# Linear attention and eight experts on one core: the step order up to chunk 7 written anew, and when expert 3's scales and the raw tiles are worked on

## The chip, the cores and the metric

The kernel runs on one core of a Trainium2 chip as one program. The metric is the device time of one execution in microseconds (us). Names of engines: PE is TensorE (PEld its weight loads), DVE is VectorE, ACT is ScalarE, POOL is GpSimd, SP is SyncE, which here only issues DMAs.

## The reference

Two stages follow each other. The first is gated linear attention over 4 batches, 8 heads, 768 tokens and 48 channels a head; the second passes its output through 8 experts, weighted by a Sinkhorn-normalised gate:

```python
def _attn_ref(q, k, v, alpha):              # each [4, 8, 768, 48]
    for t in range(S):
        state = alpha[:, :, t, :, None] * state + einsum('bhd,bhe->bhde', k[:, :, t], v[:, :, t])
        y[:, :, t] = einsum('bhd,bhde->bhe', q[:, :, t], state)

def _moe_ref(x, w_gate, w1, w2):            # x [3072, 384], w1 [8, 384, 1024], w2 [8, 1024, 384]
    logits = x @ w_gate
    P = exp(logits - logits.max())
    for _ in range(8):
        P /= P.sum(1, keepdims=True) + 1e-09
        P /= P.sum(0, keepdims=True) + 1e-09
        P *= N / E
    for e in range(E):
        out += P[:, e:e + 1] * (maximum(x @ w1[e], 0.0) @ w2[e])
```

## The kernel before

**Attention.** The 3072 tokens (4 batches of 768) are 24 chunks of 128 and 12 units of 256 (two chunks). Chunks 0 to 3 are worked directly (`direct_chunk`, 12 steps each); from unit 2 on, `attn_block` (16 steps and a DMA step) prepares a unit: it loads q, alpha and k (`qt`, `al`, `kt`), forms products within groups of 16 tokens on POOL (`tmp`), sums them on DVE into `AB`, multiplies decays into `qt`, `kt`, `al`, and writes all of it to DRAM and back in another layout (`ks`, `qs`, `ds`, `As`, then `KN`, `QN`, `DN`, `an`). That write-back is the last step, 13 DMAs on SP. `attn_decays` turns `DN` on PE (`psd`) into the decay tables (`dT`, `q32`, `k32` and others); `attn_chunk` (5 steps) turns K and Q (`psk`, `psq`), multiplies in the tables (`decq`, `deck`, on DVE), forms the scores on PE (`psl`), copies them out on ACT (`A`), and `attn_tail` forms the output (`psy`), scales it by its maximum (`mx`, then four one-column operations to `s_t`, all on DVE, then `ys` on ACT), turns it (`psx`) and splits it into two half-precision parts (`xT`: ACT the high part, DVE the low one). A chunk is done for the experts when its `xT` is written. Names carry batch and chunk: chunk 4 is `0_4`, chunk 5 `0_5`, chunk 6 `1_0`, chunk 7 `1_1`, chunk 8 `1_2`; blocks of units 2, 3, 4 are `0_2`, `1_0`, `1_1`.

**Experts.** Each product of the second stage is three half-precision matmuls (`PASSES`). `moe_tile` takes 256 tokens (512 later) of one expert: 8 hidden tiles (`ps1`, 9 matmuls each, evacuated by ACT into `h0` and by DVE into `h1`), then an output tile for each 128 tokens (`ps2`, 24 matmuls). PSUM holds four such tiles. `load_expert` loads a weight matrix, squares it on ACT (`junk`, four pieces), sums over partitions on PE (`pst_w1`, `pst_w2`), derives a power of two on DVE (`root_scale`, six small operations) and splits the weights in four pieces (`w10`/`w11`, `w20`/`w21`).

**Order.** Experts 0 to 2 (NA = 3) run beside the attention: their tiles stand in the list `filler`, and `fill(us)` takes that many us of matmuls from it. Their outputs go to DRAM unscaled (`evac_raw`, tensors `raw0` to `raw2`), since the gate is known only after all chunks. Up to chunk 7 (and two steps of chunk 8) the order is written out by hand in the string START: `c3` is a step of chunk 3, `b2` one of unit 2's block, `w1` one of expert 1's weights, `d2` the decays of unit 2, `g` the gate's weights, `f` a `fill(0.45)`, which does nothing while the list is empty. A capital letter gives more work to POOL: in `B`, the first product of the block's last level (`tmp8`, 128x1536) runs on POOL and not on DVE; in `W`, a piece's low part is formed on POOL. PE always keeps the order in which the program is written; up to the end of the Sinkhorn phase so do DVE, ACT, POOL and SP (`hold`). From chunk 8 on, a planner interleaves steps with `fill(4.7 / 2)`.

**After the attention** comes the Sinkhorn phase, a chain of small DVE operations and one matmul an iteration (`pssk`) among filler; then the rest of the list, in which expert 3's weights are scaled, one step after each `fill(1.0)`; then experts 3 to 7 in turn. Expert 3 reads all three raw tiles of its 128 tokens back (`ri`, pool `rp` of three buffers) and adds them, scaled by the gate (`evac_first`); the others only add their own output (`evac_add`).

Of the kernel before, what the change touches and what calls it, by code (L numbers as in the profile page):

```python
# [23 lines left out]
def tile_gla_moe(ctx: ExitStack, tc: tile.TileContext, q, k, v, alpha, wg, w1, w2, out):  # L24
    nc = tc.nc
    B, H, S, D = q.shape
    NT, DM = out.shape
    E, _, FF = w1.shape
    P = 128
# [6 lines left out]
    NP = H // 2  # L36
    DP = 64
    OFF = 28
    START = 'c0 c1 f c0 f f f c1 W0 w0 f f c0 f c1 f f f f f w0 c0 f f W0 w0 f f f f f f c0 f f f c1 w0 f w0 c1 c0 f f f f w1 f w0 f f w0 f f w0 c1 w0 f w0 W1 f f c0 c2 f f f c2 f c1 f g c1 c0 c3 f f c1 f f W0 c0 f W0 f w0 f c2 c3 f f c1 f c1 f W0 c0 g c2 f w1 f f c0 W1 f f c3 w1 g f f c2 W1 f c3 c2 c1 f f f c3 w1 w0 f f f c2 f f f w1 c3 f f f c2 f f f f f f f w1 c3 f f W1 c3 f w1 f f f f f f f f f c3 w1 f c2 w1 b2 w1 w1 f f f W1 f c2 f f b2 f f f f f f c2 f f f f f f B2 f w1 f B2 f c2 c3 f f f b2 f f f f c3 c3 f f f f B2 f B2 b2 f f f f f f f f B2 f f f f f f f f f f f f f b2 f f b2 f f B2 B2 B2 f f f f b2 f f B2 f f f f f f f f f f f f f f f f c4 d2 f f f f f c4 f f f B3 b3 f f b3 c0 c4 f f f f f b3 b3 b3 b3 b3 f f f f f b3 w2 c5 f f f f f b3 f f f f f b3 w2 c4 f f f f f f b3 f f f f f b3 w2 c5 f f f f f b3 f f f f f b3 w2 c4 f f f f f f b3 f f f f f w2 c5 f f f f f f f f f f w2 d3 c6 f f f f f f f f f f f b4 w2 c5 f f f f f b4 f f f f f b4 w2 c6 f f f f f b4 f f f f f f b4 w2 c5 f f f f f b4 f f f f f b4 w2 c6 f f f f f b4 f f f f f b4 w2 c7 f f f f f f b4 f f f f f b4 w2 c6 f f f f f b4 f f f f f b4 w2 c7 f f f f f f b4 f f f f f b4 w2 c6 f f f f f b4 f f f f f w2 c7 f f f f f f f f f f f w2 d4 c8 f f f f f f f f f f b5 c7 f f f f f b5 f f f f f f b5 c8 f f f f f b5 f f f f f b5 c7 f f f f f b5 f f f f f b5'.split()
    FILL = 4.7  # L40
    NA = 3

# [20 lines left out]
    VE, SE, GE, SP = (Held(x) for x in (nc.vector, nc.scalar, nc.gpsimd, nc.sync))  # L63
# [4 lines left out]
    def tr(out_, in_, idn):  # L68
# [4 lines left out]
    sm = ctx.enter_context(tc.tile_pool(name="sm", bufs=4))  # L73
# [40 lines left out]
    def root_scale(sq, target, nm):  # L114

        g = sm.tile([P, 1], F32, tag="rs_g", name=f"g_{nm}")
        VE.tensor_reduce(g, sq, axis=AX.X, op=ALU.add)
        VE.tensor_scalar_max(g, g, 1e-30)
        p = sm.tile([P, 1], F32, tag="rs_p", name=f"p_{nm}")
        VE.tensor_scalar(p.bitcast(I32), g.bitcast(I32), 24, 23,  # L120
                         op0=ALU.logical_shift_right, op1=ALU.logical_shift_left)
        VE.tensor_scalar_mul(p, p, 2.0 ** 64)
        r = sm.tile([P, 1], F32, tag="rs_r", name=f"r_{nm}")
        VE.tensor_scalar(r.bitcast(I32), p.bitcast(I32), EXPM, None, op0=ALU.bitwise_xor)
        sc = sm.tile([P, 1], F32, tag="rs_s", name=f"s_{nm}")
        VE.tensor_scalar_mul(sc, r, target / 2)
        return p, sc
# [32 lines left out]
    def load_expert(e, pool, res):  # L160

        todo, pws = [], []
        for nm, w, target, C, W in (("w1", w1, W1T, KT_, FF), ("w2", w2, W2T, FT, DM)):
            src = w[e].rearrange("(c p) f -> p c f", p=P)
            hl = [(wpa[0] if e == NA - 1 else wp).tile([P, C, W], F16, tag=f"{nm}{i}", name=f"{nm}{i}_{e}")
                  for i in range(2)]
            res.append(hl)
            hl = [x.rearrange("p c w -> p (c w)") for x in hl]
            if pool is None:

                r = 1 if nm == "w1" else 2
# [535 lines left out]
    def fill(us):  # L707
        owed[0] += us
        while owed[0] > 0 and filler:
            try:  # L710
                owed[0] -= next(filler[0])
            except StopIteration:
                filler.pop(0)
        if not filler:
            owed[0] = 0.0

    def advance(gen, n):
        for _ in range(n):
            next(gen, None)
# [162 lines left out]
    advance(w3_, 99)
    hold[0] = False
# [3 lines left out]

    T = 512

    def evac_first(e, tt, ps):  # L890
        for i in range(NA):
            r = rp.tile([P, DM], F32, tag="raw", name=f"ri{i}_{tt}")
            SP.dma_start(r, raw[i][tt * P:(tt + 1) * P])
            pt = sm.tile([P, 1], F32, tag="pe0", name=f"pe{i}_{tt}")
            VE.tensor_mul(pt, PR[:, tt, i:i + 1], wsc[:, i:i + 1])
            if i == 0:
                SE.activation(acc[:, tt], r, AF.Copy, scale=pt)
            else:
                VE.scalar_tensor_tensor(acc[:, tt], r, pt, acc[:, tt], op0=ALU.mult, op1=ALU.add)
# [44 lines left out]
```

## Time and profile before

| | us |
|---|---|
| three runs, median (lowest to highest) | 1843.33 (1843.16 to 1844.97) |
| the profiled execution | 1843.05 |
| its span, first to last instruction | 1841.3 |
| around the span | 1.75 |
| PE busy | 1745.6 |
| DVE, ACT, POOL busy | 840.4, 541.9, 297.4 |

A row of the timeline gives start, duration, engine, line, operation, output<-inputs, shape and count, and in brackets how long that engine had sat idle just before and what released it. Line numbers say little here, since nearly all operations are recorded through the two helpers at lines 57 and 66; tiles are told apart by name and place in time. A row of the table by stages gives the stage, its length, and for each engine busy time and instruction count; PEclk is the granted PE clock as a share of full speed.

### The profile page before, as it was taken

How to read it: one execution, taken by the hardware profiler on the slowest of the kernel's cores; microseconds unless marked ns; L12 is line 12 of the kernel's file. 1: busy time of each engine (PE TensorE's matmuls, PEld its weight loads, DVE VectorE, ACT ScalarE, POOL GpSimd, SP SyncE). 2: the span in 40 equal slices, each digit the busy share in tenths (PEclk: the TensorE clock that was granted, in tenths of full speed). 3: DMA queues.
4: the chain of work that ended last, by engine and by line, in shares of the span. 5: the costliest groups of instructions: out<-in, count | busy, mean ns of one | idle time of the engine just before them, and what ended most of it. 6: DMA issues, size and time to landing. Idle time of an engine off the chain costs nothing.

```text
span 1841.3 us, 34101 instructions
## 1 busy us (share of the span) xinstructions
PE 1745.6 (95%) x14774; PEld 1132.8 (62%) x14774; DVE 840.4 (46%) x1851; ACT 541.9 (29%) x1221; POOL 297.4 (16%) x270
## 2 busy tenths in 40 slices
PE   5899488999999999998999999999999999999999
PEld 5776466777777777776554555555555555555555
DVE  6465576666566556336465233222422242222222
ACT  5453243334333333325442123111411121111111
POOL 1124444445335424200000000000000000000000
PEclk9999598999999999999999999999999999999999
DMA  6114503431330432022362002000200000000000
GB/s 174 37 41 97 145 21 82 98 74 44 94 93 19 102 94 62 25 95 78 123 195 86 1 1 69 1 1 1 69 1 1 1 1 1 1 1 19 34 18 35
DMA packets 148198, 98.13 MB, mean 53 GB/s; under 512 B 107216, under 2 KB 138192, under 8 KB 148048
## 3 DMA queue, kind: packets, MB, share of 16 engines
q1 hardware_dynamic: 148048, 95.95, 18.8%
q8 instruction: 116, 1.90, 0.4%
q14 instruction: 34, 0.28, 0.1%
HBM read 67.63 MB, written 28.30 MB: 52 GB/s over the span
## 4 chain that ended last, share of the span: by engine, by line
PE 78%; DVE 10%; ACT 4%; DMA 4%; issue 2%; POOL 1%; SPq 0%; ACTq 0%; DVEq 0%; POOLq 0%
PE ps L66 70%; PE psy L66 3%; PE psl L66 2%; DMA ri<-raw 2%; DVE AB L57 2%; POOL tmp L57 1%; DVE tmp L57 1%; DVE deck L57 1%; DVE decq L57 1%; DVE h L57 1%; PE pss L66 1%; DVE w L57 1%; ACT junk L57 1%; ACT w L57 1%; ACT A L57 1%
## 5 line engine op out<-in xcount | busy, mean ns | idle before, releaser
L66 PE MATMUL ps<-xT,w 128*128 128x256 f16 (+2 forms) x4824 | 777.8, 320 | 16.8 <-DVE h L57 13.1
L66 PE MATMUL ps<-w,h 128*128 128x384 f16 x4608 | 774.1, 327 | 10.7 <-DVE h L57 9.8
L66 PEld LDWEIGHTS <-w 128*128 128x128 f16 x4824 | 467.7, 99 | 304.7 <-issue 20.1
L66 PEld LDWEIGHTS <-h 128*128 128x128 f16 x4608 | 450.0, 98 | 306.0 <-issue 9.7
L57 ACT ACTIVATE h<-ps 128x256 f16<-128x256 f32 (+2 forms) x536 | 251.6, 475 | 800.1 <-PE ps L66 799.6
L57 DVE SCALAR_TENSOR_TENSOR h<-ps,h 128x256 f16<-128x256 f32 (+2 forms) x536 | 280.9, 537 | 434.6 <-ACT h L57 434.2
L57 DVE SCALAR_TENSOR_TENSOR acc<-ps,pe,acc 128x384 f32<-128x384 f32 x120 | 74.1, 617 | 307.6 <-PE ps L66 307.6
L57 POOL TENSOR_TENSOR tmp<-qt,kt 128x768 f32<-128x768 f32 (+2 forms) x81 | 141.5, 1752 | 153.1 <-DVE AB L57 66.0
L57 DVE TENSOR_REDUCE AB<-tmp 128x16 f32<-128x768 f32 (+2 forms) x90 | 81.1, 902 | 42.0 <-POOL tmp L57 41.8
L57 ACT COPY r<-ps 128x384 f32<-128x384 f32 x72 | 34.4, 477 | 149.4 <-PE ps L66 139.7
L57 ACT COPY A<-psl 16x128 f32<-16x128 f32 (+4 forms) x164 | 52.5, 327 | 53.4 <-PE psl L66 51.9
L66 PE MATMUL psy<-vn,A 128*128 128x48 f32 x384 | 58.2, 283 | 1.7 <-issue 1.7
L66 PE MATMUL psl<-Tq,Tk 48*32 48x16 f32 (+3 forms) x2752 | 46.1, 191 | 13.9 <-DVE A L57 6.0
L66 PEld LDWEIGHTS psy<-vn,A 128*128 128x128 f32 x384 | 54.9, 209 | 2.1 <-issue 2.0
L66 PEld LDWEIGHTS psl<-Tq,Tk 48*32 48x32 f32 (+2 forms) x2752 | 40.7, 114 | 23.9 <-issue 8.7
L57 ACT ACTIVATE ys<-psy,s_t 128x384 f32<-128x384 f32 x24 | 14.0, 581 | 104.0 <-DVE s_t L57 79.4
L57 POOL TENSOR_TENSOR kt<-kt,al 128x384 f32<-128x384 f32 x40 | 41.1, 1028 | 2.6
L57 POOL TENSOR_TENSOR A<-an,mask 128x1024 f32<-128x1024 f32 x20 | 40.0, 2000 | 0.0
L57 DVE TENSOR_TENSOR qt<-qt,al 128x384 f32<-128x384 f32 (+1 forms) x50 | 39.6, 792 | 0.0
L57 DVE SCALAR_TENSOR_TENSOR acc<-ri,pe,acc 128x384 f32<-128x384 f32 x48 | 29.5, 616 | 21.4 <-DMA ri<-raw 18.3
L57 DVE TENSOR_REDUCE mx<-psy 128x1 f32<-128x384 f32 x24 | 13.3, 555 | 56.7 <-PE psy L66 56.7
L66 PE MATMUL psy<-ST,Tq 128*128 128x96 f32 x160 | 35.6, 306 | 2.9 <-DVE lg L57 1.8
(160 smaller groups left out, 965.0 us busy)
## 6 DMA issues: line engine op xcount, KB each, us to landing
raw<-r SPq DMA_DIRECT2D x72, 192.0 KB, 1.9
ri<-raw SPq DMA_DIRECT2D x72, 192.0 KB, 2.4
w1f<-in_moe_w_dram SPq DMA_DIRECT2D x5, 1536.0 KB, 6.4
w2f<-in_moe_w_dram SPq DMA_DIRECT2D x5, 1536.0 KB, 7.3
vn<-in_v_dram SPq DMA_DIRECT2D x24, 192.0 KB, 3.6
xT<-in_moe_w_dram SPq DMA_DIRECT2D x6, 768.0 KB, 6.7
out_dram<-acc SPq DMA_DIRECT2D x24, 192.0 KB, 1.9
qt<-in_q_dram SPq DMA_DIRECT2D x10, 384.0 KB, 5.4
```

The costliest lines, as they stand in the source:

```text
L57: r = f(*a, **k_)
L66: tc.keep_in_program_order(nc.tensor.matmul(out_, lhsT, rhs, start=start, stop=stop))
```

## The change

START is new up to chunk 7: the same steps (571 entries before, 640 after, the difference being `f`), in another order and with other capitals (one `B3` before, nine now; `B4` and `B5` are new). The work taken from `filler` within START is the same 111.36 us by the kernel's own count, and each engine's instructions are the same in kind. SP's order within START is unchanged.

Expert 3's weights take one step in each Sinkhorn iteration after the fourth, and the rest as soon as no tile of expert 0 is left in the list. Before the Sinkhorn phase the list, but for the tile in work, is sorted by expert. From expert 3 on, two empty steps stand between the squares and the sum on PE; from expert 4 on, eight stand before the squares. Experts 3, 4 and 5 read back and add one raw tile each (of experts 0, 1, 2). Squares are taken of weights times 2^16, and the power of two that undoes it is adapted (2^48 for 2^64): no instruction more or less.

```diff
-    START = 'c0 c1 f c0 f f f c1 W0 w0 f f c0 f c1 ...
+    START = 'c0 c0 f f c1 c0 f c1 f f f f f f c1 f ...
...
-        VE.tensor_scalar_mul(p, p, 2.0 ** 64)
+        VE.tensor_scalar_mul(p, p, 2.0 ** 48)
...
+        if e > NA:
+            yield from [None] * 8
         for nm, target, hl, cut, a in todo:
...
-                SE.activation(junk, a[i], AF.Square, accum_out=ss[:, i:i + 1])
+                SE.activation(junk, a[i], AF.Square, scale=2.0 ** 16, accum_out=ss[:, i:i + 1])
                 if i % 2:
                     yield
+            if e >= NA:
+                yield from [None] * 2
...
+    filler[1:] = sorted(filler[1:], key=lambda x: x[0])
     w3_ = load_expert(NA, wst, ws)
     advance(w3_, 2)
     for n, _ in enumerate(sinkhorn()):
         fill(2.8 if n else 4.0)
-    while len(filler) > 3:
-        fill(0.1)
+        if n > 3:
+            advance(w3_, 1)
     while filler:
-        advance(w3_, 1)
+        if all(e for e, _ in filler):
+            advance(w3_, 1)
         fill(1.0)
...
-    def evac_first(e, tt, ps):
-        for i in range(NA):
-            r = rp.tile([P, DM], F32, tag="raw", name=f"ri{i}_{tt}")
-            SP.dma_start(r, raw[i][tt * P:(tt + 1) * P])
...
+    def evac_both(e, tt, ps):
+
+        i = e - NA
+        r = rp.tile([P, DM], F32, tag="raw", name=f"ri{i}_{tt}")
+        SP.dma_start(r, raw[i][tt * P:(tt + 1) * P])
...
-            for _ in moe_tile(e, ws, t0, T, hp2, evac_first if e == NA else evac_add):
+            for _ in moe_tile(e, ws, t0, T, hp2, evac_both if e < 2 * NA else evac_add):
```

Three places where the order moved, as the built programs have it. First DVE, around chunk 4's maximum (`mx_0_4`) and the block of unit 3 (`AB1`, `qt_1_0`, `al_1_0`). Before:

```order
L57 TENSOR_REDUCE AB1_121<-tmp4_1_0_9_2614 128x16
L57 TENSOR_SCALAR lg_83<-psg_0_0_2624,p_t_0_0_912,ipwg_89 128x8
L57 TENSOR_REDUCE mx_0_4_2652<-psy_0_4_2639 128x1
L57 TENSOR_SCALAR m_t_0_4_2654<-mx_0_4_2652 128x1
L57 TENSOR_SCALAR p_t_0_4_2656<-m_t_0_4_2654 128x1
```

After:

```order
L57 TENSOR_REDUCE AB1_121<-tmp4_1_0_9_2590 128x16
L57 TENSOR_TENSOR qt_1_0_2431<-qt_1_0_2431,al_1_0_2433 128x768
L57 TENSOR_REDUCE AB1_121<-tmp1_1_0_10_2594 128x8
L57 TENSOR_TENSOR qt_1_0_2431<-qt_1_0_2431,al_1_0_2433 128x8x48
L57 TENSOR_TENSOR al_1_0_2433<-al_1_0_2433 128x8x48
L57 TENSOR_REDUCE mx_0_4_2615<-psy_0_4_2602 128x1
```

The maximum moved behind four more operations of unit 3's block. Second PE, after chunk 5's output (`psy_0_5`): unit 3's decays and chunk 6's K and Q (`psd_1_0`, `psk_1_0`, `psq_1_0`), chunk 5's last transposes (`psx_0_5`), and the first expert tile that reads chunk 5 (`ps1_0_512_0`, nine matmuls). Before:

```order
L69 MATMUL psd_1_0_2947<-ident_64,DN_117 128x16 x4
L69 MATMUL psk_1_0_2974<-ident_64,KN1_116 128x128 x4
L69 MATMUL psq_1_0_2981<-ident_64,QN1_114 128x128 x4
L69 MATMUL psx_0_5_3006<-ident_64,ys_0_5_2943 128x128 x3
L66 LDWEIGHTS w10_0_284
L66 MATMUL ps1_0_512_0_3014<-xT0_0_77,w10_0_284 128x256
```

After, `psx_0_5` and the whole first hidden tile stand ahead, and its last rows are followed by the twelve:

```order
L66 LDWEIGHTS w11_0_429
L66 MATMUL ps1_0_512_0_2963<-xT0_0_77,w11_0_429 128x256
L69 MATMUL psd_1_0_2975<-ident_64,DN_117 128x16 x4
L69 MATMUL psk_1_0_3002<-ident_64,KN1_116 128x128 x4
L69 MATMUL psq_1_0_3009<-ident_64,QN1_114 128x128 x4
```

The twelve transposes for chunk 6 moved behind chunk 5's last work. Third PE, at unit 4's decays (`psd_1_1`), against expert 2's first hidden tiles (`ps1_2_0_0` to `_7`). Before:

```order
L69 MATMUL pskn_1_1_3651<-ident_64,Tk_1_1_3365 128x128 x4
L69 MATMUL psd_1_1_3661<-ident_64,DN_117 128x16 x4
L69 MATMUL psk_1_2_3688<-ident_64,KN0_115 128x128 x4
L69 MATMUL psq_1_2_3695<-ident_64,QN0_113 128x128 x4
L66 LDWEIGHTS w10_2_2733
L66 MATMUL ps1_2_0_0_3714<-xT0_0_77,w10_2_2733 128x256
```

After:

```order
L66 MATMUL ps1_2_0_5_3744<-xT1_0_80,w10_2_2733 128x256
L66 LDWEIGHTS w11_2_2734
L66 MATMUL ps1_2_0_5_3744<-xT0_0_77,w11_2_2734 128x256
L69 MATMUL psd_1_1_3756<-ident_64,DN_117 128x16 x4
L66 LDWEIGHTS w10_2_2733
L66 MATMUL ps1_2_0_6_3783<-xT0_0_77,w10_2_2733 128x256
```

Six of expert 2's hidden tiles (54 matmuls) moved ahead of `psd_1_1`.

More of the change, by code (lines that the diff above doesn't have):

```diff
@@ L38, in tile_gla_moe @@
     OFF = 28
-    START = 'c0 c1 f c0 f f f c1 W0 w0 f f c0 f c1 f f f f f w0 c0 f f W0 w0 f f f f f f c0 f f f c1 w0 f w0 c1 c0 f f f f w1 f w0 f f w0 f f w0 c1 w0 f w0 W1 f f c0 c2 f f f c2 f c1 f g c1 c0 c3 f f c1 f f W0 c0 f W0 f w0 f c2 c3 f f c1 f c1 f W0 c0 g c2 f w1 f f c0 W1 f f c3 w1 g f f c2 W1 f c3 c2 c1 f f f c3 w1 w0 f f f c2 f f f w1 c3 f f f c2 f f f f f f f w1 c3 f f W1 c3 f w1 f f f f f f f f f c3 w1 f c2 w1 b2 w1 w1 f f f W1 f c2 f f b2 f f f f f f c2 f f f f f f B2 f w1 f B2 f c2 c3 f f f b2 f f f f c3 c3 f f f f B2 f B2 b2 f f f f f f f f B2 f f f f f f f f f f f f f b2 f f b2 f f B2 B2 B2 f f f f b2 f f B2 f f f f f f f f f f f f f f f f c4 d2 f f f f f c4 f f f B3 b3 f f b3 c0 c4 f f f f f b3 b3 b3 b3 b3 f f f f f b3 w2 c5 f f f f f b3 f f f f f b3 w2 c4 f f f f f f b3 f f f f f b3 w2 c5 f f f f f b3 f f f f f b3 w2 c4 f f f f f f b3 f f f f f w2 c5 f f f f f f f f f f w2 d3 c6 f f f f f f f f f f f b4 w2 c5 f f f f f b4 f f f f f b4 w2 c6 f f f f f b4 f f f f f f b4 w2 c5 f f f f f b4 f f f f f b4 w2 c6 f f f f f b4 f f f f f b4 w2 c7 f f f f f f b4 f f f f f b4 w2 c6 f f f f f b4 f f f f f b4 w2 c7 f f f f f f b4 f f f f f b4 w2 c6 f f f f f b4 f f f f f w2 c7 f f f f f f f f f f f w2 d4 c8 f f f f f f f f f f b5 c7 f f f f f b5 f f f f f f b5 c8 f f f f f b5 f f f f f b5 c7 f f f f f b5 f f f f f b5'.split()
@@ new lines, in tile_gla_moe @@
+    START = 'c0 c0 f f c1 c0 f c1 f f f f f f c1 f f W0 f f f f c0 f f f W0 W0 f f f f w0 f f f f f f f f f f f f f f f f f w0 c0 f c1 f W1 f f w0 f f f f f f f c1 c0 f f w0 f f w0 f f f f w0 f w0 f f f f f f w1 f w0 c1 f w0 c0 f g c2 c0 f W0 f c3 c1 c0 f f c3 f c1 f f f c0 w0 f c1 f W0 f f c1 f f c2 f W0 f f f c1 c2 w1 c2 f f f f f f f f f g c0 w1 f f c3 c2 f W1 f c3 w1 f f c2 f g f W0 f f f w1 c3 c2 f W1 f f w1 w1 f f c2 f c3 f c1 f f f f f f f c3 f f f f W1 f c3 f f f f f f f f f f W1 f f c3 c2 f f f w1 f w1 w1 f f W1 f f B2 f f b2 f f f c2 f f f f f f c2 B2 f f b2 c3 f f f f b2 f f c3 c2 B2 f f f B2 w1 f f f B2 c3 f f f f f f f f B2 f f f f f f f f f f f f b2 f f f B2 f f b2 f B2 b2 b2 f f f f f b2 f f f f f f f f f f f f c4 f f f f b3 f f f f c4 f f f d2 b3 b3 B3 b3 c4 b3 B3 f f c0 f f B3 f f f B3 f f f f f f f f w2 f f B3 f f c5 f f c4 f f f f w2 f f b3 f f f B3 f f f w2 f f w2 f f f f f f f f f f b3 f f f f f c5 f B3 f f B3 f f w2 f c5 f f f f c4 f w2 f f f f f f B3 f f f f c6 f B4 f f f w2 f f f f f f f f f f f f f f f c5 f d3 f f f f B4 f f f b4 c6 f f b4 w2 f f f f f f f f B4 f f c5 f w2 b4 w2 f w2 f f f b4 f f f f c6 f f f b4 f f f f f b4 f f f f f f c7 f f w2 f b4 f f f f f w2 c7 f b4 f f B4 f b4 w2 f f c6 f f f f f f f f f f f f B4 f f f f f f b4 f f f f f f f f f f f f f f f w2 f f f f f f B4 c6 f f f f f f f w2 f f f f c7 f f B5 f f c7 f f f f d4 f f f c8 f f b5 f f b5 f f f f f f f c7 c8 f f B5 f f f f f f B5 f f B5 f b5 f f f f f'.split()
@@ L710, in fill @@
             try:
-                owed[0] -= next(filler[0])
+                owed[0] -= next(filler[0][1])
             except StopIteration:
@@ L744, in push @@
     def push(*tiles):
-        filler.extend(moe_tile(e, wAB[e], t0, T, hp1, evac_raw) for e, t0, T in tiles)
+        filler.extend((e, moe_tile(e, wAB[e], t0, T, hp1, evac_raw)) for e, t0, T in tiles)
     steps = [0] * len(chunks)
@@ L888, in tile_gla_moe @@
     T = 512
-    def evac_first(e, tt, ps):
-        for i in range(NA):
-            r = rp.tile([P, DM], F32, tag="raw", name=f"ri{i}_{tt}")
-            SP.dma_start(r, raw[i][tt * P:(tt + 1) * P])
[L894 to L899, printed above, removed]
+    def evac_both(e, tt, ps):
+        i = e - NA
+        r = rp.tile([P, DM], F32, tag="raw", name=f"ri{i}_{tt}")
+        SP.dma_start(r, raw[i][tt * P:(tt + 1) * P])
+        pt = sm.tile([P, 1], F32, tag="pe0", name=f"pe{i}_{tt}")
+        VE.tensor_mul(pt, PR[:, tt, i:i + 1], wsc[:, i:i + 1])
+        if i == 0:
+            SE.activation(acc[:, tt], r, AF.Copy, scale=pt)
+        else:
+            VE.scalar_tensor_tensor(acc[:, tt], r, pt, acc[:, tt], op0=ALU.mult, op1=ALU.add)
         evac_add(e, tt, ps)
```

## The prediction

> **What bounds the kernel now.** I read the page's first lines, then a table by stages cut where PE's idle time changes, then the waits of PE in the poor stages, then the timeline at each long one.
>
> ```profile
> span 1841.3 us, 34101 instructions
> PE 1745.6 (95%) x14774; PEld 1132.8 (62%) x14774; DVE 840.4 (46%) x1851; ACT 541.9 (29%) x1221; POOL 297.4 (16%) x270
> ```
>
> The table's columns: stage, length, busy time and instructions of PE, PEld, DVE, ACT, POOL, granted clock, DMA share, GB/s.
>
> ```profile
> 0.00:72.00 72.00, 47.58 (x1157) 41.93 (x1158) 39.71 (x150) 34.16 (x69) 13.48 (x38) 1.00 0.50 134
> 72.00:115.00 43.00, 36.43 (x907) 28.77 (x908) 23.70 (x87) 23.02 (x61) 2.60 (x3) 0.96 0.03 8
> 115.00:162.80 47.80, 45.46 (x380) 36.56 (x377) 29.88 (x66) 16.87 (x38) 23.82 (x20) 1.00 0.27 72
> 162.80:187.00 24.20, 21.39 (x255) 16.40 (x255) 13.42 (x30) 8.99 (x28) 11.88 (x11) 0.93 0.58 148
> 187.00:199.00 12.00, 0.81 (x65) 0.69 (x64) 8.94 (x8) 1.56 (x4) 10.78 (x8) 0.62 0.52 185
> 199.00:223.50 24.50, 12.29 (x99) 10.44 (x100) 15.21 (x36) 8.76 (x25) 6.29 (x6) 0.50 0.62 137
> 223.50:245.20 21.70, 21.69 (x261) 16.61 (x261) 12.80 (x23) 9.07 (x22) 9.90 (x8) 0.91 0.05 16
> 245.20:259.20 14.00, 8.90 (x82) 7.93 (x81) 11.20 (x17) 6.81 (x17) 9.64 (x7) 0.96 0.04 15
> 259.20:277.00 17.80, 17.71 (x210) 12.86 (x209) 10.90 (x21) 6.79 (x15) 4.63 (x3) 0.84 0.14 41
> 277.00:282.60 5.60, 0.00 (x1) 0.03 (x1) 2.18 (x7) 1.89 (x3) 0.18 (x1) 0.65 0.90 202
> 282.60:299.70 17.10, 17.10 (x220) 14.17 (x221) 10.79 (x25) 5.63 (x19) 6.40 (x6) 0.82 0.54 120
> 299.70:800.00 500.30, 490.19 (x5424) 386.90 (x5425) 290.42 (x571) 175.37 (x486) 197.80 (x164) 1.00 0.27 67
> 800.00:868.00 68.00, 61.98 (x466) 45.36 (x464) 38.17 (x119) 27.54 (x60) 0.00 (x0) 1.00 0.27 94
> 868.00:985.00 117.00, 111.34 (x645) 62.63 (x645) 69.47 (x194) 52.71 (x106) 0.00 (x0) 1.00 0.54 164
> 985.00:1841.30 856.30, 852.69 (x4617) 451.56 (x4614) 263.62 (x505) 162.70 (x273) 0.00 (x0) 1.00 0.04 14
> ```
>
> PE bounds the kernel: 1745.6 of 1841.3 us, so all its idle time is 95.7 us. The change alters no matmul, and START takes as much from the list as before, so PE's work is the same; the time can only change by PE's idle time and its clock. By stage (length less PE busy) the idle time is 24.4, 6.6, 2.3, 2.8, 11.2, 12.2, 0, 5.1, 0.1, 5.6, 0, 10.1, 6.0 and 5.7; after 985 us 3.6 remain. START covers everything up to a little past 299.7. From there to 800 the planner goes on with the same list and the same state: 0. After 985 us: 0. From 115 to 162.8 the matmuls wait for unit 2's block, whose own order stays: 0. Four terms are left. SP issues START's DMAs in the same order as before; behind it, two writes of `raw2` fall behind two weight loads, and nothing reads either for many us. Of the new capitals only one moves work: unit 3's long product goes from DVE to POOL.
>
> **Term 1: chunks 4 and 5 (162.8 to 223.5).**
>
> ```profile
> 145.43 5.29 POOL L57 TENSOR_TENSOR tmp<-qt,kt 128x1536 f32<-128x1536 f32 x2 [0.49 <-DVE qt L57]
> 174.44 1.80 POOL L57 TENSOR_TENSOR tmp<-qt,kt 128x768 f32<-128x768 f32 x1 [5.15 <-DMA kt<-in_k_dram]
> 178.59 0.96 DVE L57 TENSOR_TENSOR qt<-qt,al 128x768 f32<-128x768 f32 x1
> 182.15 0.56 DVE L57 TENSOR_TENSOR al<-al 128x384 f32<-128x384 f32 x1
> 192.94 3.44 DVE L57 TENSOR_TENSOR tmp<-qt,kt 128x1536 f32<-128x1536 f32 x1
> 199.03 1.93 PE L66 MATMUL psl<-decq,deck 48*32 48x32 f32 x48 [11.22 <-DVE deck L57]
> 205.32 0.59 PE L66 MATMUL pst_w<-w1m,ones 128*128 128x4 f32 x2 [3.14 <-ACT junk L57]
> 207.74 0.74 PE L66 MATMUL psy<-ST,Tq 128*128 128x96 f32 x2 [1.83 <-DVE lg L57]
> 213.13 0.56 DVE L57 TENSOR_REDUCE mx<-psy 128x1 f32<-128x384 f32 x1 [4.44 <-PE psy L66]
> 217.18 1.11 PE L69 MATMUL psq<-ident,QN 128*128 128x128 f32 x4 [0.90 <-DVE dT L57]
> 223.51 6.86 PE L66 MATMUL ps<-xT,w 128*128 128x256 f16 x44 [2.69 <-DVE xT L57]
> ```
>
> Chunk 4's maximum now stands behind four operations of unit 3's block, which ran from 178.59 to 182.71 us: `ys` comes 4.1 us later, and behind it on ACT the copies of two hidden tiles, for which PE's expert matmuls then wait. That moves some 5 us of idle time ahead of the long wait at 199.03; it costs nothing, since that wait ends with DVE's `deck` and not with PE's matmuls. I take the wait itself as unchanged: DVE loses the 3.44 us product at 192.94 to POOL, where one of that shape takes 3.49 (5.29 for two, less the 1.80 of the smaller), so DVE's reduction now waits for POOL; the bounds are 0 and 1.8 us later, the latter being one POOL operation in the way.
>
> Behind the wait the gain is plainer. The squares (`junk`) now precede the copies of `A` on ACT, and `lg` follows the output on DVE: the idle 3.14 and 1.83 go, 4.97 together. From chunk 5's maximum (213.13) to the first expert matmul that reads chunk 5 (223.51) pass 10.4 us, with unit 3's transposes and ACT's twelve small copies in between; now these come afterwards. How long the bare chain takes, chunk 1 shows:
>
> ```profile
> 69.79 0.56 DVE L57 TENSOR_REDUCE mx<-psy 128x1 f32<-128x384 f32 x1 [6.68 <-PE psy L66]
> 73.28 0.56 DVE L57 TENSOR_TENSOR xT<-psx,xT 128x384 f16<-128x384 f32 x1 [2.18 <-ACT xT L57]
> ```
>
> That is 4.05 us from start to end. With one weight piece on ACT in between (0.96 by the nearest DVE row of that width) it is 5.1, with two 6.0. I take 5.1, a gain of 5.3. The transposes that stood inside the old gap now take PE's time behind it: 1.11 for `psq`, as much for `psk` and 0.58 for `psd` (row in term 2), 2.8. Net: 4.97 + 5.3 − 2.8 − 0.5 (for `dT`'s wait of 0.90, half kept) = **7.0**. Ends: 0, if the long wait grows by what is saved behind it, and 10.3, if the transposes hide beside the chain.
>
> **Term 2: unit 4's block and decays (245.2 to 299.7).**
>
> ```profile
> 245.16 4.09 PE L66 MATMUL ps<-xT,w 128*128 128x256 f16 x36
> 252.71 3.45 DVE L57 TENSOR_TENSOR tmp<-qt,kt 128x1536 f32<-128x1536 f32 x1
> 259.15 2.08 PE L66 MATMUL ps<-w,h 128*128 128x384 f16 x6 [5.09 <-DVE h L57]
> 282.60 0.58 PE L69 MATMUL psd<-ident,DN 16*128 16x16 f32 x4 [5.61 <-DMA DN<-ds]
> ```
>
> PE waits 5.09 us for an `h` that stands on DVE behind unit 4's long product and its reduction, and 5.61 us for the block's round trip through DRAM. In the new order the hidden tile before it no longer stands behind the reduction; the long product starts about 1.7 us earlier (one reduction) and ends near 254.9, while PE runs out of matmuls at about 252.6. A wait of 2.3 replaces the 5.09. Ahead of `psd` now stand six hidden tiles of expert 2, which need only weights and old tokens: 54 matmuls at 0.114 (4.09/36) are 6.1 us, more than 5.61, so this wait goes whole. Saved 5.09 − 2.3 + 5.61 = 8.4, less 0.9 for what else the queue shift delays: 7.5.
>
> The clock adds to it. Behind these two holes it was 0.84 and 0.82: 17.80 × 0.16 + 17.10 × 0.18 = 5.9 us lost. How far the clock recovers when a hole shrinks, one more stage tells:
>
> ```profile
> 168.00:173.00 5.00, 4.91 (x68) 3.28 (x69) 2.26 (x6) 2.61 (x8) 1.08 (x1) 0.66 0.87 228
> ```
>
> Here PE was busy 4.91 of 5.00 us and still got 0.66, so a short gap or none is no surety for a full clock. I take a quarter of the 5.9, 1.5. Term: **9.0**. Ends: 3 (the `DN` wait half covered, the other wait the same, no clock) and 13.4 (all of the clock).
>
> The Trainium skill ("TensorE: Matmul & The Clock Gate", Part 1: The HAM clock gate) says that the clock halves only after an idle window of about 3.4 us and is full again after as long a busy one. By that rule a wait of 2.3 would cost no clock, and the term would be 13.4 instead of 9.0. The row of 168 to 173 us speaks against it, 0.66 with PE idle for 0.09 us.
>
> **Term 3: the start (0 to 115).** Chunk 0 is brought ahead of chunk 1, so its `ys` ends about 4 us earlier; expert 0's weight pieces, which share ACT with it, come in between and eat about 2.6 (three pieces of 0.96, less a gap). I take **1.5**. No trace shows this order; the nearest row is the idle 6.6 us of the stage from 72 to 115, which can go or come twice: ends −6.6 and +6.6.
>
> **Term 4: expert 3's scales and raw tiles (800 to 985).**
>
> ```profile
> 850.47 0.39 PE L66 MATMUL pst_w<-w1m,ones 128*128 128x4 f32 x2 [1.63 <-ACT junk L57]
> 860.46 0.39 PE L66 MATMUL pst_w<-w2m,ones 128*128 128x4 f32 x2 [2.75 <-ACT junk L57]
> 982.73 0.66 PE L66 MATMUL ps<-w,h 128*128 128x384 f16 x3 [1.52 <-DVE h L57]
> L57 DVE SCALAR_TENSOR_TENSOR acc<-ri,pe,acc 128x384 f32<-128x384 f32 x48 | 29.5, 616 | 21.4 <-DMA ri<-raw 18.3
> ```
>
> The sums over partitions stand right behind the squares, so PE waits 1.63 and 2.75 for ACT. Two empty steps between them put two `fill(1.0)`, some 2 us of matmuls, in the gap: the first wait goes and of the second 0.75 may stay, 3.6 gained. While expert 3 adds three raw tiles a token tile, PE idles 5.7 us, the longest time (1.52) for an `h` that DVE evacuates late, DVE having waited 18.3 for `ri` to land. With one tile in three a third of that idle is left: 3.8 gained. Experts 4 and 5 get 24 of these additions each, 24 × 0.616 = 14.8 us of DVE; DVE is busy 263.62 us of the last 856.3, 31%, so they hide. Expert 3's scales inside the Sinkhorn phase put small DVE operations into its chain, but filler covers PE there. Term: **7.4**. Ends: 3.6 (raw part nothing) and 11.7 (all idle of both stages).
>
> **Sum.** 7.0 + 9.0 + 1.5 + 7.4 = 24.9. The sum is against the profiled execution: 1843.05, that is the span of 1841.3 and 1.75 around it, 0.3 below the median of 1843.33. Prediction: 1843.05 − 24.9 = **1818**.
>
> **The rivals.**
> - The clock recovers wholly once no hole is long: 13.4 in term 2, 1813.7. For it: 1.00 in the stages with many short waits (299.7 to 800). Against: 0.66 at 168 to 173.
> - All terms at their upper ends: 10.3 + 13.4 + 6.6 + 11.7 = 42, 1801. Every wait would have to vanish with nothing late behind it.
> - The new order in START gains only its surest part: 0 + 3 + 0 + 7.4, 1832.6. For it: between 187 and 199 DVE (8.94 of 12.00) and POOL (10.78) set the pace, not PE; what PE saves before or after, it may wait out at the next `deck`.
> - Nothing: START's gain is paid back at the next hole and the later waits are only moved: 1843.
> - Slower: the clock. From 187 to 223.5 it fell to 0.50 behind the 11.2 us hole. PE's work from 162.8 to 299.7, in us of full clock, is busy time times clock, 19.9 + 0.5 + 6.1 + 19.7 + 8.5 + 14.9 + 14.0 = 83.6. If waits cut it so finely that the clock stays at half to chunk 8, it takes 167.2 instead of 136.9, +30.3; less terms 3 and 4 (8.9), 1864. It ends slower than before from 62 of the 83.6 us at half clock on: 83.6 + 62 = 136.9 + 8.9. Against: the present order, with longer holes, recovers to 0.91 from 223.5 on.
>
> **How the numbers follow.** The forecast, 1812 to 1828: 0.42. The clock rival 0.12, all ends up 0.08, surest part only 0.20, nothing 0.09, slower 0.09. Leaving out the extremes on both sides, the range is 1804 to 1840. About 0.2% (3.7 us) is what a measurement of this kernel tells from no change; faster by more has 0.42 + 0.12 + 0.08 + 0.20 = 0.82, within it 0.09, slower 0.09.
>
> **What would show it.** Term 1: `deck`'s wait at about 11 us still there, no wait of `pst_w` for `junk` nor of `psy` for `lg` behind it, and some 5 us from chunk 5's `mx` to its `xT`. Term 2: no wait of unit 4's `psd` for `DN`, about 2 us for the `h` before it, and a clock above 0.85 up to chunk 8. Term 3: PE idle from 0 to 115 near 29.5 (31.0 before). Term 4: PE idle near 2.4 in the Sinkhorn phase, near 2 beside expert 3, and no new idle beside experts 4 and 5. Wrong it would be if the long wait grows because unit 3's product on POOL becomes what `AB` and then `deck` wait for, or if the clock stays at half.

## The result and the profile after

The changed kernel takes 1803.07 us (median of four runs, 1801.93 to 1803.55) against 1844.15 for the kernel before (1843.16 to 1846.79): ratio 0.9774, 95% interval 0.9757 to 0.9791, 41 us faster. The forecast was 1818 with a range from 1804; the time ends below it, where the prediction had put the case "all terms at their upper ends" (1801).

The page of the changed kernel's profile; the profiled execution took 1802.96 us:

```profile
span 1801.2 us, 34072 instructions
PE 1741.3 (97%) x14774; PEld 1132.8 (63%) x14774; DVE 832.3 (46%) x1850; ACT 541.3 (30%) x1221; POOL 298.1 (17%) x271
```

PE's instructions are the same in number. Its idle time fell from 95.7 to 59.9 us (35.8 less), and its busy time from 1745.6 to 1741.3. The two make up the 40.1 us of span. The mean granted clock of the whole execution is about the same (0.982 before, 0.981 after); most of the busy time that went lies in the third stage below (72.23 to 68.22), where the clock is 1.00 instead of 0.90. Where the 40.1 us lie is seen when both kernels are cut at the same events: start, unit 2's `psd`, chunk 6's `mx`, the reduction of unit 5's long product, the first and the last `pssk`, end. Columns as in the prediction's table. Before:

```profile
0.00:162.78 162.78, 129.46 (x2439) 107.24 (x2440) 93.29 (x302) 74.04 (x165) 39.89 (x60) 0.99 0.31 82
162.78:244.36 81.58, 55.36 (x674) 43.64 (x675) 49.60 (x93) 28.39 (x78) 38.01 (x31) 0.75 0.45 117
244.36:327.37 83.01, 72.23 (x735) 56.92 (x734) 55.16 (x100) 30.74 (x78) 39.80 (x31) 0.90 0.23 57
327.37:822.60 495.23, 484.75 (x5375) 381.43 (x5374) 277.47 (x560) 171.05 (x475) 179.71 (x149) 1.00 0.29 74
822.60:846.60 24.00, 23.00 (x173) 17.33 (x172) 19.31 (x67) 6.08 (x16) 0.00 (x0) 1.00 0.07 26
846.60:1841.30 994.70, 980.78 (x5386) 526.27 (x5384) 345.58 (x732) 231.57 (x410) 0.00 (x0) 1.00 0.11 34
```

After:

```profile
0.00:155.67 155.67, 128.67 (x2449) 108.53 (x2449) 93.61 (x302) 73.98 (x165) 39.93 (x60) 0.91 0.32 86
155.67:228.18 72.51, 58.15 (x660) 45.66 (x660) 45.29 (x92) 30.01 (x82) 40.59 (x32) 0.74 0.50 131
228.18:298.22 70.04, 68.22 (x753) 54.64 (x752) 50.34 (x100) 29.03 (x75) 37.54 (x31) 1.00 0.29 71
298.22:792.60 494.38, 483.93 (x5363) 380.19 (x5361) 275.49 (x560) 170.21 (x474) 179.99 (x149) 1.00 0.29 73
792.60:816.70 24.10, 22.77 (x174) 17.36 (x173) 19.59 (x68) 9.68 (x23) 0.00 (x0) 1.00 0.07 25
816.70:1801.20 984.50, 979.55 (x5386) 526.47 (x5385) 347.95 (x731) 228.42 (x402) 0.00 (x0) 1.00 0.11 34
```

The lengths differ by 7.1, 9.1, 13.0, 0.9, -0.1 and 10.2 us. These are the prediction's term 3 (1.5), term 1 (7.0), term 2 (9.0), the planner (0), the Sinkhorn phase (0) and term 4 (7.4). Every one of the four stages gained more than its term. That the last one's surplus belongs to term 4 does not hold; the runs behind the Sinkhorn phase show it below.

### The profile page after: what moved, and what is told of

The parts are those of the page before. It is cut to its first block, busy times and chain, and to the rows that moved or that the text cites. A ratio compares the mean times of both kernels' runs of the same rounds, so it can differ in the third digit from the quotient of the medians.

```text
span 1801.2 us, 34072 instructions
## 1 busy us (share of the span) xinstructions
PE 1741.3 (97%) x14774; PEld 1132.8 (63%) x14774; DVE 832.3 (46%) x1850; ACT 541.3 (30%) x1221; POOL 298.1 (17%) x271
## 4 chain that ended last, share of the span: by engine, by line
PE 81%; DVE 9%; ACT 3%; DMA 2%; issue 2%; POOL 2%; SPq 0%; ACTq 0%; POOLq 0%; DVEq 0%
PE ps L66 73%; PE psy L66 3%; PE psl L66 3%; DVE AB L57 1%; POOL tmp L57 1%; DMA ri<-raw 1%; DVE deck L57 1%; DVE h L57 1%; DVE decq L57 1%; DVE tmp L57 1%; PE pss L66 1%; ACT w L57 1%; DVE w L57 0%; DVE qt L57 0%; ACT h L57 0%
## 5 line engine op out<-in xcount | busy, mean ns | idle before, releaser
L66 PE MATMUL ps<-xT,w 128*128 128x256 f16 (+2 forms) x4824 | 778.1, 321 | 11.7 <-DVE h L57 9.0
L57 ACT COPY A<-psl 16x128 f32<-16x128 f32 (+4 forms) x164 | 52.3, 326 | 43.2 <-PE psl L66 41.7
L66 PEld LDWEIGHTS psl<-Tq,Tk 48*32 48x32 f32 (+2 forms) x2752 | 40.1, 114 | 23.8 <-DVE A L57 9.9
L57 DVE TENSOR_TENSOR pe<-PR,wsc 128x1 f32<-128x1 f32 x192 | 29.7, 158 | 14.8 <-ACT acc L57 9.6
```

Of the source, the lines that this page charges most:

```text
L57: r = f(*a, **k_)
L66: tc.keep_in_program_order(nc.tensor.matmul(out_, lhsT, rhs, start=start, stop=stop))
```

## The experiments

Each kernel was timed against the kernel before on its own chip, in five rounds; microseconds below are 1843 times one less the ratio. "START" is the string of steps.

**Adding the change up from the front.** Three kernels carry more and more of the new START, with everything behind START as before; a fourth has only what stands behind START.

```diff
start_to_chunk4:  START = new up to and with the first c4, old from the d2 behind it on
start_to_chunk7:  START = new up to the fills ahead of the first c7, old from that c7 on
start_only:       START = new
rest_only:        START = old; list sorted, scales, empty steps and evac_both as changed
```

> The new START up to chunk 4's first step, the old from there on, the rest as before. Theory: the 7.1 us by which unit 2's decays come earlier in the changed kernel stay to the end, 1837. Rival: the next long wait (the one for deck, 11.2 us) swallows them, since it hangs on unit 3's block and not on PE: 1843 to 1844. The prediction's term for this stretch gives 1842.7.

> The new START up to just ahead of chunk 7's first step, the old from there on, the rest as before. Theory: terms for the start and for chunks 4 and 5 as the traces show them (7.1 + 9.1) and none of unit 4's: 1828. Rival: the early part only shifts idle time into unit 4's two waits: above 1835; or unit 4's gain hangs on the early part alone, below 1822.

> The new START alone; everything behind it as before. Theory: the stages' gains belong to START and add up, so the 30.0 us by which the Sinkhorn phase starts earlier in the changed kernel appear whole: 1844 - 30 = 1814. Rival: the prediction's own three START terms (7.0 + 9.0 + 1.5) were right and the rest came from sorting the queue: 1826.

> The old START with all the rest of the change (sorted queue, scales in the Sinkhorn phase, empty steps, one raw tile for each of experts 3, 4 and 5). Theory: it is worth the 10.1 us that the traces show behind the Sinkhorn phase, 1834. Rival: the prediction's 7.4 us, 1836.7; if the rest only pays with the new START, under 4 us, above 1840.

| kernel | median us | ratio (95%) | gain us | what its last step adds |
|---|---|---|---|---|
| start_to_chunk4 | 1837.51 | 0.9980 (0.9969 to 0.9992) | 3.7 | 3.7 |
| start_to_chunk7 | 1827.47 | 0.9924 (0.9911 to 0.9936) | 14.0 | 10.3 |
| start_only | 1810.20 | 0.9830 (0.9812 to 0.9847) | 31.3 | 17.3 |
| the whole change | 1803.07 | 0.9774 (0.9757 to 0.9791) | 41.7 | 10.4 |
| rest_only | 1835.35 | 0.9964 (0.9952 to 0.9977) | 6.6 | |

START is worth 31 us (28 to 35), as the two traces said, and not the 17.5 of the prediction's terms 1 to 3. The largest piece is the last one of START, from chunk 7's first step on: 17 us where term 2 had 9. The entries of the last column but the first are differences of two measurements and hold to some 3 to 4.5 us either way. The start by itself brings 3.7 (1.5 to 5.7) and not 7.1: half the theory, and the rival that the next long wait swallows it holds for the other half. The rest by itself brings 6.6 (4.2 to 8.8); on the new START 10.4.

**Why an early start was half swallowed.** In start_to_chunk4 unit 2's `psd` starts 5.4 us earlier than before (157.37), but chunk 5's first scores only 1.9 (197.15 against 199.03). Its timeline, of PE and DVE:

```profile
157.37 0.41 PE L69 MATMUL psd<-ident,DN 16*128 16x16 f32 x4 [4.59 <-DMA DN<-ds]
170.63 0.95 DVE L57 TENSOR_REDUCE AB<-tmp 128x16 f32<-128x768 f32 x1 [1.95 <-POOL tmp L57]
176.71 0.95 DVE L57 TENSOR_TENSOR qt<-qt,al 128x768 f32<-128x768 f32 x1
197.15 1.93 PE L66 MATMUL psl<-decq,deck 48*32 48x32 f32 x48 [10.65 <-DVE deck L57]
```

Unit 3's block stands still on DVE from 171.6 to 176.7: chunk 4's maximum and two expert copies come between. Two kernels move two of the block's steps ahead of that maximum, as the change does:

```diff
-... B3 b3 f f b3 c0 c4 f f f f f b3 b3 b3 b3 b3 ...
+... B3 b3 f f b3 b3 b3 c0 c4 f f f f f b3 b3 b3 ...
```

> Before, with one change: two steps of unit 3's block (its first three DVE operations behind AB) stand ahead of chunk 4's maximum instead of behind it. Theory: unit 3's chain sets when deck comes, and the maximum holds it up by some 2 us (AB ends 177.2, qt starts 178.6): 1843 - 2 = 1841. Rival: chunk 4's ys comes 4 us later and the experts' matmuls behind it are lost, 1843 or above.

> The new START up to chunk 4's first step (as in start_to_chunk4) and the same move of two steps of unit 3's block ahead of chunk 4's maximum. In start_to_chunk4 unit 2's decays came 5.4 us earlier and deck of chunk 5 only 1.9: between AB (170.6) and qt (176.7) stood the maximum and two expert copies that wait for PE. Theory: with the block ahead the early gain survives, 1837.5 - 4 = 1833.5. Rival: another wait takes them, 1837.

block_ahead_of_max measured 0.9997 (0.9988 to 1.0006): nothing. start_to_chunk4_block_ahead measured 0.9968 (0.9956 to 0.9981), 5.9 us, 2.2 more than without the move, with intervals that overlap. The theory that this one move decides it falls. Its trace shows what came in the place of the wait:

```profile
174.97 1.08 PE L69 MATMUL pskn<-ident,Tk 128*128 128x128 f32 x4 [5.72 <-DVE lg L57]
180.69 1.00 DVE L57 TENSOR_REDUCE AB<-tmp 128x8 f32<-128x384 f32 x2
195.19 1.93 PE L66 MATMUL psl<-decq,deck 48*32 48x32 f32 x48 [4.37 <-DVE deck L57]
```

PE now waits 5.72 us for `lg`, which moved back with the maximum; the matmuls behind it come late, so do the copies that DVE has to make of them, and unit 3's next reduction (180.69) stands behind these copies. In the changed kernel `pskn` starts at 170.62 with no wait for `lg`. Whether that is all that is needed was not tried; it stays open.

**Unit 4's round trip: hole and clock.** late_decays covers the hole in the kernel before with the fills that followed it; early_decays opens it again in the changed kernel.

```diff
late_decays (from before)
-... w2 d4 c8 f f f f f f f f f f b5 c7 ...
+... w2 f f f f f f f f f f d4 c8 b5 c7 ...
early_decays (from the changed kernel)
-... c7 f f B5 f f c7 f f f f d4 f f f c8 ...
+... c7 d4 f f B5 f f c7 f f f f f f f c8 ...
```

> Before, with one change: unit 4's decays (d4) stand behind the ten fills that followed them, so that 4.5 us of matmuls cover the 5.6 us in which DN travels. Theory: 4.5 us of idle time go and the clock behind it comes back from 0.82 (3.1 us): 1843 - 7.6 = 1835.5. Rival 1: idle time only, 1838.5. Rival 2: chunk 8's scores, which those fills had covered, now wait as long: 1843.

> The changed kernel with unit 4's decays (d4) moved ahead by one step of chunk 7, so that PE reaches psd some 5 us before DN lands. Theory: the hole costs its length and the clock behind it, 4.9 + 3.1 (17.1 us at 0.82 instead of 1.00, as before): 1811. Rival 1: the hole alone, 1808. Rival 2: nothing, since the work that it delays is taken up later, 1803.

late_decays measured 0.9962 (0.9950 to 0.9975), 7.0 us (4.6 to 9.2). Idle time alone (4.5) lies just below that interval and the theory of idle time and clock (7.6) inside it. The table by stages of before at that place, and below it that of late_decays:

```profile
277.00:282.60 5.60, 0.00 (x1) 0.03 (x1) 2.18 (x7) 1.89 (x3) 0.18 (x1) 0.65 0.90 202
282.60:285.00 2.40, 2.40 (x13) 2.30 (x14) 1.18 (x8) 1.53 (x9) 0.00 (x0) 0.50 1.09 217
285.00:300.00 15.00, 15.00 (x211) 12.04 (x210) 9.91 (x17) 4.31 (x12) 6.70 (x6) 0.87 0.44 102
```

```profile
277.00:282.00 5.00, 4.00 (x38) 3.44 (x36) 2.84 (x10) 2.99 (x7) 0.18 (x1) 1.00 0.86 210
282.00:285.00 3.00, 2.51 (x21) 1.70 (x18) 2.19 (x12) 1.46 (x10) 0.00 (x0) 1.00 0.91 154
285.00:300.00 15.00, 14.47 (x210) 10.57 (x211) 8.79 (x14) 5.34 (x15) 8.69 (x8) 1.00 0.55 125
```

PE idles 2.0 us in these stages instead of 5.6. With no wait over 1 us the clock stays at 1.00; with the hole it was 0.50 and then 0.87 (2.40 × 0.50 + 15.0 × 0.13 = 3.2 us lost). The 3.6 us of idle time and the 3.2 of clock make 6.8, beside 7.0 measured. early_decays measured 1807.31, ratio 0.9806 (0.9794 to 0.9819), so 5.9 us slower than the changed kernel by the ratios. Its `psd` in the timeline, and then the table for the hole and the stage behind it:

```profile
260.52 0.58 PE L69 MATMUL psd<-ident,DN 16*128 16x16 f32 x4 [5.00 <-DMA DN<-ds]
```

```profile
255.00:260.50 5.50, 0.53 (x5) 0.29 (x5) 1.17 (x5) 1.06 (x2) 1.14 (x3) 0.67 0.88 179
260.50:265.00 4.50, 4.48 (x29) 3.66 (x30) 1.72 (x10) 1.97 (x11) 0.00 (x0) 0.65 1.09 187
```

The hole is the expected 5.0 us, and the clock falls behind it, but for some 5 us and not for 17: 4.48 × 0.35 = 1.6 us. The 5.9 lie between the two expectations (5 and 8), and with their interval the run does not tell them apart; the clock's own price is read from the records here and from late_decays.

**Unit 3's long product.**

```diff
-... B3 ... (nine steps of unit 3's block)
+... b3 ...
```

> The changed kernel with unit 3's long product on DVE again. The stage from unit 2's decays to chunk 5's scores took 36.3 us before and 35.4 after, although PE's wait for deck went from 11.2 to 0.8. Theory: this stage hangs on unit 3's chain through POOL and DVE, and the product costs the same on either: 1803 +- 1. Rival 1: the product on POOL is what shortened it, so 3.3 us come back: 1806.5. Rival 2: POOL was late, 1801.

1801.36 us, 0.9773 (0.9759 to 0.9788), against 0.9774 (0.9757 to 0.9791): no difference, but this comparison holds only to some 4 us either way, so it excludes none of the three expectations. The trace does not bear out the theory's reason. From it, unit 2's `psd` and chunk 5's first scores:

```profile
156.88 0.42 PE L69 MATMUL psd<-ident,DN 16*128 16x16 f32 x4
189.60 1.42 PE L66 MATMUL psl<-decq,deck 48*32 48x32 f32 x48 [1.32 <-DVE deck L57]
```

The product takes 1.75 us on DVE here (row in the last section) and 3.51 on POOL in the changed kernel, and the scores come 32.72 us after `psd` instead of 35.36. So by this one execution the stage does hang on unit 3's chain, but the product does not cost the same on either engine; rival 2, that POOL was late, is nearer. Its span is 3.4 us shorter than the changed kernel's (1797.8 against 1801.2), but other executions of the same kernel took as long as 1803.21 us, so how much of this stays in the time is open.

**Behind the Sinkhorn phase.** Three parts of the change, each by itself in the kernel before (the eight empty steps from expert 4 on and the scale of the squares were not tried by themselves):

```diff
raw_only:              evac_first if e == NA  ->  evac_both if e < 2 * NA
empty_only:            + if e >= NA: yield from [None] * 2      (ahead of pst)
sort_and_scales_only:  + filler[1:] = sorted(...); w3_ steps from Sinkhorn iteration 4 on
```

> Before, with one change: experts 3, 4 and 5 read back and add one raw tile each. Theory: all of PE's idle time beside expert 3 goes (5.7 us), 1838.5. Rival: one load of three keeps its share of it, as predicted (3.8), 1840.3; or the idle time moves to experts 4 and 5, 1844.

> Before, with one change: two empty steps between the squares and the sum on PE from expert 3 on. Theory: the two waits of 1.63 and 2.75 us go but for 0.75, 1844 - 3.6 = 1840.5. Rival: PE waits as long for something else that stood behind the squares (the split weights of expert 3), 1844.

> Before, with one change: the list sorted by expert and expert 3's scales inside the Sinkhorn phase; no empty steps, three raw tiles in expert 3 as before. Theory: it gains next to nothing by itself, since the waits for the squares stay: 1842 to 1843. Rival: it is what empties PE's waits behind the Sinkhorn phase, 1839 or less.

raw_only 1837.47, 0.9969 (0.9957 to 0.9981), 5.7 us; empty_only 1837.22, 0.9971 (0.9960 to 0.9983), 5.3 us; sort_and_scales_only 1842.81, 0.9995 (0.9986 to 1.0004), nothing. By the run the raw tiles bring as much as all of PE's idle time beside expert 3 (5.7, between 3.5 and 7.9). The trace of raw_only says less: in the stretch that answers to 868 to 985 us of before PE idles 2.2 us instead of 5.7, and the longest wait of these is still for `h`:

```profile
866.00:978.70 112.70, 110.48 (x645) 63.08 (x645) 46.96 (x124) 53.21 (x107) 0.00 (x0) 1.00 0.35 111
936.74 4.13 PE L66 MATMUL ps<-xT,w 128*128 128x512 f16 x18 [1.82 <-DVE h L57]
```

The empty steps bring at least what the two waits were; in the trace of empty_only PE waits for `junk` no more. In that of sort_and_scales_only the waits for `junk` are halved (2.2 instead of 4.4 us) and those for `h` are longer (7.1 instead of 5.8).

Whether these parts are worth 6.6 or 10.4 together, the traces tell better than the runs. From the last `pssk` to the end of the stage with expert 3, in this order before, rest_only, start_only and the changed kernel:

```profile
846.60:985.00 138.40, 128.09 (x771) 74.71 (x770) 81.96 (x228) 68.87 (x137) 0.00 (x0) 1.00 0.50 153
844.70:976.00 131.30, 128.84 (x771) 75.56 (x771) 59.83 (x158) 66.97 (x130) 0.00 (x0) 0.99 0.35 110
812.60:948.00 135.40, 128.34 (x772) 74.87 (x772) 81.41 (x227) 68.30 (x135) 0.00 (x0) 1.00 0.49 156
816.70:945.00 128.30, 126.94 (x772) 75.16 (x772) 59.75 (x158) 66.69 (x130) 0.00 (x0) 1.00 0.36 113
```

In these single executions the parts bring 7.1 us on the old START and 7.1 on the new one. The other 3.0 us come in start_only, whose code from there on is that of before. Kernels with that code but other orders in START need between 991.5 us (start_only) and 997.8 (start_to_chunk4_block_ahead) from the last `pssk` to the end; whether the order ahead sets this, or chance, was not tried. In the changed kernel the addition's group, then from the timeline the one wait left for the squares, then the stage from expert 4 on read:

```profile
L57 DVE SCALAR_TENSOR_TENSOR acc<-ri,pe,acc 128x384 f32<-128x384 f32 x48 | 29.3, 611 | 0.2 <-DMA ri<-raw 0.2
```

```profile
827.83 0.39 PE L66 MATMUL pst_w<-w2m,ones 128*128 128x4 f32 x2 [0.90 <-ACT junk L57]
```

```profile
945.00:1801.20 856.20, 852.60 (x4616) 451.31 (x4614) 288.20 (x574) 161.72 (x272) 0.00 (x0) 1.00 0.07 22
```

DVE's waits for `ri` went from 18.3 us to 0.2. In the last 856 us DVE has 24.6 us more work (288.20 against 263.62) and PE idles 3.6 us as before.

## Why the prediction was wrong in size

The traces gained some 15 us more than the 24.9 of the sum: 5.6 in term 3's stages, 4.0 in term 2's, 2.1 in term 1's, 2.8 in term 4's and 0.8 in between. The mechanism, idle time and clock around holes, was right; the sizes below were not.

**Term 2 is a step that failed: 9.0 predicted, 13.0 in the traces and 17.3 by the runs.** It had 5.09 and 5.61 us of idle time, took off a new wait of 2.3 and 0.9 of delays, and gave the clock a quarter of the 5.9 us that it loses there. Neither deduction came true before chunk 8's scores, and the quarter was the largest error: all of the 5.9 came back. All of the idle time and all of the clock would be 5.09 + 5.61 + 5.9 = 16.6. The changed kernel from chunk 6's `mx` to past chunk 8's scores (268.53), with an earlier stage above it:

```profile
161.00:181.00 20.00, 15.66 (x114) 12.19 (x115) 11.11 (x21) 4.05 (x11) 11.00 (x11) 0.50 0.21 58
228.00:280.00 52.00, 52.00 (x631) 42.35 (x629) 35.64 (x77) 23.97 (x63) 24.08 (x21) 1.00 0.37 87
```

PE is busy for all of the 52 us, at full clock. The wait for `h` that was to stay at 2.3 did not come there. The long product takes 1.75 us in the changed kernel and not 3.45, which by the prediction's own working leaves 0.6 of the 2.3; that the product, and not the new order of the matmuls, is the cause was not tried. (The 252.6 us at which PE was to run out of matmuls stands in no row; before, its last one ahead of that wait ends at 249.97 + 4.09 = 254.06.) Two smaller waits for `h` come later, behind chunk 8's scores:

```profile
282.80 2.12 PE L66 MATMUL ps<-xT,w 128*128 128x256 f16 x18 [0.50 <-DVE h L57]
286.24 1.14 PE L66 MATMUL ps<-w,h 128*128 128x384 f16 x6 [1.32 <-DVE h L57]
```

The traces' 13.0 is 16.6 less these 1.8 and less 18 more matmuls that lie in that stage after the change (753 against 735, some 2 us at 0.114), to within 0.2. That a clock that recovers wholly was only a rival (0.12) cost this term most: the row of 168 to 173 us (busy, yet 0.66) had been read as if the clock did not recover in general, but it stood right behind two waits, of 1.71 us (`psd`) and 1.21 (`psl`).

**Term 3: 1.5 predicted, 7.1 in the traces, 3.7 alone on the chip.** Two steps failed. The weight pieces on ACT do not eat the gain of chunk 0's earlier turn: `mx` of chunk 0 comes at 44.80 instead of 49.81, that of chunk 1 still 2.4 earlier and that of chunk 2 4.8 (115.39 against 120.24), where the term had 1.5. And 115 to 162.8 was set at 0 "since unit 2's block stays": the matmuls ahead of unit 2's `psd` were moved so that its wait of 1.71 us for `DN` went, another 2.3 in all. By itself on the chip, 3.7 is within the prediction's ends (-6.6 and +6.6) and 7.1 is not: with the old order behind it, about half of what the start gains is lost again.

**Term 1: 7.0 predicted, 9.1 in the traces, 10.3 by the runs; the working behind the long wait holds, with two signs missed.** Rows of the changed kernel:

```profile
191.03 1.42 PE L66 MATMUL psl<-decq,deck 48*32 48x32 f32 x48 [0.83 <-DVE deck L57]
193.57 0.39 PE L66 MATMUL pst_w<-w1m,ones 128*128 128x4 f32 x2 [1.11 <-ACT junk L57]
200.84 0.56 DVE L57 TENSOR_REDUCE mx<-psy 128x1 f32<-128x384 f32 x1 [1.42 <-PE psy L66]
205.54 0.55 DVE L57 TENSOR_TENSOR xT<-psx,xT 128x384 f16<-128x384 f32 x1
206.15 1.87 PE L66 MATMUL ps<-xT,w 128*128 128x256 f16 x8 [0.89 <-DVE xT L57]
207.95 0.60 PE L69 MATMUL psd<-ident,DN 16*128 16x16 f32 x4
```

From `mx` to `xT` it is 5.25 us, predicted 5.1. The wait of 11.22 for `deck` shrank to 0.83, where the prediction named "about 11 us still there" as the sign; and `pst_w` still waits 1.11 for `junk`, where no wait was to be left. Yet the stage that ends with it is only 0.9 us shorter (unit 2's `psd` to these scores: 36.25 before, 35.36 after): the idle time went into smaller pieces and into the clock, which is 0.50 from 161 to 181 us. From the scores to chunk 5's `mx` 4.3 are gained (4.97 predicted), from there to the first expert matmul that waits for chunk 5's `xT` 5.1 (5.3 predicted), and behind it 1.2 are lost and not 3.3: the transposes were counted too dear. The stage hangs on unit 3's block, as the term assumed, but the 3.44 us product that it moved to POOL was not all work: beside POOL's `A` and `tmp` it took 3.44; in unit3_product_on_dve, where POOL had nothing running when it began, it took 1.75, and the scores come 2.6 us sooner after `psd`.

**Term 4: 7.4 predicted; its stages gain 10.2 in the traces, but 7.1 of that comes from its parts.** The term holds: 7.1 on either START, 6.6 by rest_only. "A third of that idle is left" is what raw_only by itself shows (2.2 of 5.7); with the empty steps and the scales beside it, in the changed kernel, next to nothing is left (two waits of 0.23). The wait behind the empty steps was forecast at 0.75 and is 0.90. That experts 4 and 5 hide their additions held. What the prediction missed is that START would shorten this stage too, by some 3 us in start_only's trace: it had put START's worth behind 299.7 us at 0. Why it does stays open.

Nearly all misses point one way. What was expected to come back in the place of a gain was counted too high (4.4 of clock and, net, 1.4 of the 3.2 deducted in term 2, 2.6 of weight pieces in term 3, 2.1 of transposes in term 1), and stretches that looked untouched were put at 0 and gained 2.3 and some 3 us. The case in which all upper ends hold had been taken as a coincidence of four, though one habit of counting made most of it: the stages' 9.1, 13.0, 7.1 and 10.2 stand close to its 10.3, 13.4, 6.6 and 11.7.

## What to carry to other kernels

Where a hole of PE is filled with matmuls that do not wait for its chain, count the idle time and the lost clock behind it nearly whole (late_decays: 3.6 and 3.2 us of a hole of 5.6). Before a duration is carried into a new place, ask whether it was work or a wait recorded inside the instruction: compare it with the shortest of the same shape. Time that is gained early is worth only what the next chain lets through: it has to be checked against the chain that sets the next long wait, here unit 3's block on POOL and DVE. When a stage's gain is put down to a change, look at the same stage in a kernel without that change: of the 10.2 us behind the Sinkhorn phase 3 came without its parts.

## What was not expected of the hardware

**A DVE product of two inputs took twice as long beside POOL.** Before, POOL and then DVE, around unit 4's long product (quoted in the prediction at 252.71, 3.45 us):

```profile
252.63 1.91 POOL L57 TENSOR_TENSOR A<-an,mask 128x1024 f32<-128x1024 f32 x1
254.50 3.31 POOL L57 TENSOR_TENSOR tmp<-qt,kt 128x768 f32<-128x768 f32 x1
256.08 2.02 DVE L57 TENSOR_TENSOR decq<-Tq,q 128x256 f32<-128x256 f32 x1
258.02 0.41 DVE L57 TENSOR_TENSOR deck<-Tk,k 128x256 f32<-128x256 f32 x1
```

The same product in the changed kernel, and in a second row that of unit 3 in unit3_product_on_dve. In both POOL had nothing running when it began; in the second POOL's `deck` starts 0.6 us before the product ends and takes 1.12 us instead of 0.62:

```profile
234.51 1.75 DVE L57 TENSOR_TENSOR tmp<-qt,kt 128x1536 f32<-128x1536 f32 x1
```

```profile
184.53 1.75 DVE L57 TENSOR_TENSOR tmp<-qt,kt 128x1536 f32<-128x1536 f32 x1
```

The four times fit operations that take turns: POOL's `A` until 254.5, then 1.7 us of DVE's product until 256.1, then 1.8 of POOL's `tmp` (1.80 alone) until 257.8, then 0.4 of `decq`, which had begun at 256.08. The Trainium skill ("SBUF — State Buffer", section "SBUF: two separate sides") says this: a DVE operation with two inputs in SBUF and a GpSimd operation that reads SBUF take the shared ports as an exclusive lock for a whole instruction, and the other blocks; the rows agree. The prediction took the 3.45 as work, and 1.7 of its new wait of 2.3 us rested on it.

**The clock stayed at half without a long wait.** From 161 to 181 us in the changed kernel it is 0.50, with PE busy 15.66 of 20 us and no wait over 2.1 us (it is 0.66 in the same window of unit3_product_on_dve), whereas between 228 and 280 us, with PE always busy, it is 1.00. The Trainium skill ("TensorE: Matmul & The Clock Gate", Part 1: The HAM clock gate) has the clock full again after some 3.4 us of sustained work and halved after an idle window as long; it also tells of a kernel in which frequent short idles made the clock go to and fro. The second stage and late_decays agree with the rule of the window; the first stage does not: even where PE is busy for 6 us on end, the clock stays at half.

```profile
167.00:170.00 3.00, 3.00 (x16) 3.00 (x16) 1.28 (x2) 0.00 (x0) 1.68 (x1) 0.50 0.00 0
170.00:173.00 3.00, 3.00 (x17) 2.50 (x17) 1.89 (x3) 0.00 (x0) 2.00 (x2) 0.50 0.00 0
```

What keeps the clock down there was not tried.
